# Batch 0 of a windowed-attention and SiLU-MLP kernel: scores of each head by its own half of the rows, q without padding, the first layer of tile 0 in halves of d_ff, and one more O group by DMA

## The chip, the core and the metric

The kernel runs on one core of a Trainium2 chip. The metric is the device time of one execution in microseconds (us); shorter is better. The profiles come from the hardware profiler, which records every instruction of each engine: TensorE (PE, and PEld for its weight loads), VectorE (DVE), ScalarE (ACT), GpSimd (POOL), and SyncE (SP), which here only issues DMAs.

## What is computed

Causal attention with a window of 64 positions over 8 batches of 8 heads (576 positions, head size 64), then a two-layer MLP with SiLU over all 4608 rows.

```
scores = (q @ k.T) / sqrt(64)              # per batch and head, 576 x 576
scores = where(0 <= i - j < 64, scores, -1e9)
attn   = softmax(scores)
O      = attn @ v                          # -> x: 4608 rows of 512 (8 heads x 64)
h      = x @ w_in                          # 512 -> 2048
out    = (h * sigmoid(h)) @ w_out          # 2048 -> 512, float32
```

## The kernel before

**Attention.** Heads go in pairs (`pj` = 0 to 3), one head on partitions 0 to 63 and the other on 64 to 127. q and k are turned by TensorE (`turn_heads`, L299, a pair of matmuls on the two 64-column halves of the array; `turn_twos`, L308) and copied from PSUM to SBUF ("lifts": `lift_q` L321, `lift_k` L327, `lift_twos` L314); later batches are turned by DMA transposes on SP's queue (L260), and DVE spreads q from the tile `raw` (L268). `kt` holds k for the pair, and `qbd` holds q padded: of each head only its own 64 partitions are filled, the others are zero, so that one matmul of 128 contraction rows and 128 columns gives both heads' scores for 64 queries against 128 keys. The zeros of both buffers of `qbd` are written once by ACT (`clear_q`, L215).

Nine blocks of 64 queries make three groups (`g`) of three blocks. For a pair and a group in batch 0, `scores_idle` fills one PSUM bank: first a matmul of the identity with a bias (L356, 384 columns), which masks, then three score matmuls (L361). ACT takes the exponential of 384 columns (L367). Other batches leave the bias out (`scores`, L349), and DVE multiplies with a mask (L370). Then `values` (L375) multiplies with v and its column of ones, DVE inverts the sums (L381) and scales (`normal_both` L410, or ACT L414, in batch 0; `normal` L387 in batches 1 and 2; `normal_rows` L404 from batch 3 on). O is turned into `bridge`, the MLP's input, in three ways: by matmuls with 64 columns (`back_both`, L420) in batch 0, by three matmuls of a 64-wide identity (`back`, L431) and a copy (L436) for each pair and group in batches 1 and 2, and by one DMA transpose for the four pairs of a group (`turn_o`, L425) from batch 3 on.

**MLP.** Nine tiles of 512 rows. The first layer of a tile is 64 matmuls (L440: 16 blocks `ft` of d_ff by 4 blocks of d_model) with a SiLU per `ft` on ACT (L446); the second layer is 64 matmuls of 512 columns (L449), a copy out (L455) and a store. Tile 0 begins before batch 0 is done: its first layer is made for rows 0 to 191, all 16 `ft`, and then for rows 192 to 511 (`PARTS`).

**Order.** The order of instructions on each engine comes from a planner in the kernel (`Plan`): every operation is added with a class, an engine or two, a guessed cost and its dependencies, and a list scheduler with ranks per class picks the next one for each engine. The hardware then runs each engine's list strictly in this order. PSUM has eight banks, four named `at` (attention) and four `mp` (MLP). In the first microseconds TensorE runs matmuls with no use, "warm" fillers (L680), wherever the plan has nothing else for it. All loads from DRAM except the first two go over POOL's queue, in one order: q, k and v of batch 0, w_in in 8 chunks (L278), batch 1, w_out in 8 chunks (L284), and the other batches.

Of the kernel before, what the change touches and what calls it, by code (L numbers as in the profile page):

```python
# [8 lines left out]
FP32 = mybir.dt.float32  # L9
# [102 lines left out]
def kernel(ctx, tc, q, k, v, w_in, w_out, out):  # L112
    nc = tc.nc
# [14 lines left out]
    NN, NNB, NE, NOB, NOT, NGT = 8, 8, 14, 6, 4, NFT + 3  # L128
    PARTS = {0: [(0, 192), (192, TT)]}
    NXQ, NXK, NXO = 4, 2, 3  # L130
# [23 lines left out]
    vv = [keep.tile([128, H * NB + 1, D + 2], BF16, name=f"vv{i}") for i in range(NK)]  # L154
    es = [keep.tile([128, 3, 2, 64], BF16, name=f"e{i}") for i in range(NE)]
    rcs = [keep.tile([128, 3, 2], FP32, name=f"rc{i}") for i in range(NRC)]
# [55 lines left out]

    def clear_q(i, hh):
        r = slice(64 - 64 * hh, 128 - 64 * hh)
        nc.scalar.copy(out=qbd[i][r, :, hh].bitcast(FP32), in_=zero[r].unsqueeze(2).to_broadcast([64, NP, S // 2]))  # L215

    def clear_ob(i):
# [5 lines left out]
    c_zero = p.add("one", {"DVE": 0.1}, lambda _: nc.vector.memset(zero, 0.0))  # L223
    c_q = {i: [p.add("first", {"ACT": 1.0}, lambda e, i=i, hh=hh: clear_q(i, hh), [c_zero]) for hh in range(2)]
           for i in range(NK)}
    c_twoi = p.add("late", {"DVE": 0.3}, const_twoi, [c_ident])
# [65 lines left out]

    def turn_heads(op, w, hs):

        pst = at_bf16(op).rearrange("x (m p) -> x m p", m=NM)
        heads = natbs[w].rearrange("p (h m d) -> p h m d", h=2, m=NM)
        for m in range(NM):
            for hh in hs:
                nc.tensor.matmul(  # L299
                    pst[64 * hh:64 * hh + 64, m], lhsT=heads[:, hh, m], rhs=ident[0:NR, 0:NR],  # L300
                    is_transpose=True, start=(m == 0), stop=(m == NM - 1),
                )
# [15 lines left out]

    def lift_q(e, op, b, pj, hh):
        r = slice(64 * hh, 64 * hh + 64)  # L320
        copies[e](  # L321
            out=qbd[b % NK][r, pj, hh].rearrange("x (p m) -> x p m", m=NM),
            in_=at_bf16(op)[r].rearrange("x (m p) -> x p m", m=NM),
        )

    def lift_k(e, op, b, pj):
        copies[e](  # L327
            out=kt[b % NK][:, 64 + pj * S:64 + (pj + 1) * S].rearrange("x (p m) -> x p m", m=NM),
            in_=at_bf16(op).rearrange("x (m p) -> x p m", m=NM),
        )  # L330

# [21 lines left out]

    def scores_idle(op, b, pj, g):

        nc.tensor.matmul(  # L356
            banks[op["bank"]][:, 0:384], lhsT=ident,
            rhs=(bias0 if g == 0 else bias).rearrange("k x h i -> k (x h i)"), start=True, stop=False)
        for x in range(3):
            t = 3 * g + x  # L360
            nc.tensor.matmul(  # L361
                at_sp(op)[:, x], lhsT=kt[b % NK][:, pj * S + t * 64:pj * S + t * 64 + 128],
                rhs=qbd[b % NK][:, pj, :, t * 64:t * 64 + 64], start=False, stop=(x == 2),
            )

    def expo(op, n):
        nc.scalar.activation(out=es[n % NE], in_=at_sp(op), func=ACTF.Exp, scale=scale)  # L367

    def masking(n, g):
# [114 lines left out]
    def add_batch_qk(b):  # L484
        pool = "at" if b else "all"
        slot, parts = {}, {0: [], 1: []}
        for pj in range(NP):
            kq_done[(b, pj)] = []
            busy = s_last.get((b - NK, pj), []) + ([c_k[b % NK]] if b < NK else [])
            for kk in range(2):  # L490
# [35 lines left out]
                else:  # L526
                    ca = [p.add("dma", {"POOL": 0.66}, lambda _, w=w, pj=pj, kk=kk: load_cast(w, b, pj, kk),
                                [natb_free.get(w)], dma=0.55 if b else 0.75)]
                by = {"ACT": 0.64, "DVE": 0.75}
                li = []  # L530

                for hs in ([(0,), (1,)] if b == 0 and not kk else [(0, 1)]):
                    twos = b > 0 and not kk
                    us = 0.27 if twos else 0.35 * len(hs)
                    tu = p.add("turn", {"PE": us}, None, ca + [c_ident] + busy, lat=0.1, pool=pool, b=b)
                    tu["fn"] = lambda _, tu=tu, w=w, hs=hs, twos=twos: turn_twos(tu, w) if twos else turn_heads(tu, w, hs)
                    if kk:
                        tu["until"] = [p.add("lift", by, lambda e, tu=tu, pj=pj: lift_k(e, tu, b, pj), [tu] + busy, b=b)]
                    elif twos:
                        for hh, r in [(0, 0), (0, 1), (1, 0), (1, 1)]:  # L540
                            tu["until"].append(p.add("lift", {"ACT": 0.44, "DVE": 0.43}, lambda e, tu=tu, pj=pj, hh=hh, r=r:
                                                     lift_twos(e, tu, b, pj, hh, r), [tu] + busy + tu["until"], b=b))
                    else:
                        for hh in hs:
                            tu["until"].append(p.add("lift", by, lambda e, tu=tu, pj=pj, hh=hh: lift_q(e, tu, b, pj, hh),
                                                     [tu] + busy + tu["until"], b=b))
                    li += tu["until"]
                natb_free[w] = tu
                kq_done[(b, pj)] += li
            if b < NIV:  # L550
# [17 lines left out]
    def add_batch_attention(b):  # L568
        pv_last[b], o_rows = [], []
        pool = "at" if b else "all"  # L570
        for g, pj in [(g, pj) for pj in range(NP) for g in range(NG)] if b < NPM else [(g, pj) for g in range(NG) for pj in range(NP)]:
# [3 lines left out]
                if b == 0:  # L575
                    pool = "at" if pj >= 2 and g else "all"
                s = p.add("s" + ahead, {"PE": 0.17 if b else 0.4}, None,
                          kq_done[(b, pj)] + g_pv[n - NE:n - NE + 1] * (n >= NE) + ([] if b else c_bias) + c_q.get(b, []),
                          lat=0.1, gate=scores_may_run, pool=pool, b=b)
                s["fn"] = lambda _, s=s, pj=pj, g=g: (scores if b else scores_idle)(s, b, pj, g)  # L580
                s_last[(b, pj)] = [s]
                ex = p.add("exp" + ahead, {"ACT": 0.5}, lambda _, s=s, n=n: expo(s, n), [s], table="exp", b=b)
                s["until"] = [ex]
                exps.setdefault(b, []).append(ex)
                ma = ex
                if b:
                    ma = p.add("mask", {"DVE": 0.37}, lambda _, n=n, g=g: masking(n, g), [ex, *c_mask], b=b)
                pv = p.add("pv" + ahead, {"PE": 0.17}, None,
                           [ma] + v_done[(b, pj)] + g_back[n - NOB:n - NOB + 1] * (n >= NOB and 0 < b < NXO), lat=0.1, pool=pool, b=b)
                pv["fn"] = lambda _, pv=pv, n=n, pj=pj, g=g: values(pv, n, b, pj, g)  # L590
# [4 lines left out]
                by = {"DVE": 0.37}  # L595
                if b >= NXO:
                    no = [p.add("norm" + ahead, by, lambda e, pv=pv, n=n, hh=hh: normal_rows(pv, n, hh),
                                [rc] + xo.get(n // NP - 2 * NOX, []), b=b) for hh in range(2)]
                    g_norm.append(no[1])
                    pv["until"] = no  # L600
                    o_rows += no
                    if pj == NP - 1:
                        xo[n // NP] = [p.add("xo", {"SP": 1.4}, lambda _, n=n, g=g: turn_o(n, b, g), o_rows, dma=1.6)]
                        o_done[NG * b + g] = xo[n // NP]
                        o_rows = []
                    g_back.append(None)
                    continue
# [19 lines left out]
    def add_tile(j):  # L627
        gt = {}
        parts = PARTS.get(j, [(0, TT)])
        for ft in range(NFT):  # L630
            gt[ft] = (n_gt[0] % NGT, [])
            n_gt[0] += 1
        left = NFT * NDC * len(parts)
        for lo, hi in parts:
            have = [op for i in range((j * TT + hi + 191) // 192) for op in o_done[i]]
            for ft in range(NFT):
                g, si = gt[ft]
                bank = None
                for c in range(NDC):
                    op = p.add("moe", {"PE": 0.0036 + (hi - lo) / 2400}, None,  # L640
                               have + [win[ft // 2]] + (exps[0] if j == 0 else []), lat=0.1,
                               pool=None if c else "mp")
                    bank = bank or op
                    op["fn"] = lambda _, bank=bank, ft=ft, c=c, lo=lo, hi=hi: first_layer(bank, j, ft, c, lo, hi)
                    moe.append((op, 1, left if left % (NFT * NDC) == 0 else -1))
                    left -= 1
                si.append(p.add("silu", {"ACT": 0.18 + (hi - lo) * 0.00083}, lambda _, bank=bank, g=g, lo=lo, hi=hi:
                                silu(bank, g, lo, hi), [op] + free_gt.get(g, []), table="silu"))
                bank["until"] = [si[-1]]
# [35 lines left out]
    for f in range(8):  # L685
        win.append(p.add("dma", {"POOL": 0.8}, lambda _, f=f: load_w_in(f), dma=1.33))
    add_batch_attention(0)

    p.add("prime", {"ACT": 0.2}, lambda _: nc.scalar.activation(out=spare, in_=zero, func=ACTF.Silu), [c_zero] + exps[0],
          table="silu")  # L690
    n_tile = 0
    for b in range(1, B):
# [43 lines left out]
```

## Time and profile before

| | us |
|---|---|
| median of 5 runs | 315.72 |
| lowest and highest | 315.37, 318.21 |
| the profiled execution's own time | 315.77 |
| its span in the profile | 313.7 |
| first matmul of the MLP (L440) starts | 22.09 |
| first matmul of the second layer of tile 0 (L449) starts | 42.23 |
| TensorE busy | 307.8 |
| ACT, DVE busy | 192.5, 158.4 |

The profiled execution spends 315.77 - 313.7 = 2.07 us outside the span. In the timelines each line has the start in us from the span's start, the busy time in us, the engine, the line of the kernel, the operation, out<-in by tile names, sizes, and how many instructions were merged; in brackets stands the idle time of the engine before it and what ended it. Matmuls overlap in their pipeline, so the busy time of a group is longer than the distance from its start to the next start; that distance is what TensorE spends on it. A matmul's weight load is a separate instruction (PEld) and runs beside earlier matmuls.

### The profile page before, as it was taken

The page shows a single profiled execution, that of the slowest core. Times are in us where ns is not written, and L with a number is a line of the kernel's source. Part 1 is how long each engine was busy: PE and PEld are TensorE (multiplying, and loading weights), DVE is VectorE, ACT ScalarE, POOL GpSimd, SP SyncE. Part 2 cuts the span into 40 slices and gives each one's busy share as a digit, 9 for nine tenths or more (in the row PEclk, how much of TensorE's full clock was granted, in tenths as well). Part 3 has the DMA queues.
Part 4 walks back from the last instruction along what each step waited for, and adds up shares of the span by engine and source line. Part 5 has one row for each costly group of instructions (what it writes and reads, how often), then busy time and mean ns, then how long its engine had stood idle before and what let it go on. Part 6 is the DMA issues. An engine that isn't in the chain of part 4 may idle for free.

```text
span 313.7 us, 6059 instructions
## 1 busy us (share of the span) xinstructions
PE 307.8 (98%) x2235; PEld 167.9 (54%) x2235; DVE 158.4 (50%) x471; ACT 192.5 (61%) x374; POOL 119.1 (38%) x159
## 2 busy tenths in 40 slices
PE   8999999999999999999999999999999999999995
PEld 4778666545665556545654464446444444444444
DVE  4894838945689898990895089408810000000000
ACT  8898686889867666277617761876186136316611
POOL 8956859576657769672455000000000000000000
PEclk9999999999999999999999999999999999999999
DMA  9999999999999999999999955200520110020011
GB/s 143 159 195 188 182 201 163 118 236 143 156 187 163 155 153 163 154 180 157 156 178 193 157 83 119 59 0 36 117 60 2 67 67 2 25 76 33 2 67 67
DMA packets 137308, 37.31 MB, mean 119 GB/s; under 512 B 121664, under 2 KB 132800, under 8 KB 137280
## 3 DMA queue, kind: packets, MB, share of 16 engines
q0 software_dynamic: 95712, 18.06, 74.8%
q1 hardware_dynamic: 41568, 18.88, 33.8%
q8 instruction: 17, 0.28, 0.4%
q14 instruction: 11, 0.09, 0.1%
HBM read 36.70 MB, written 9.44 MB: 147 GB/s over the span
## 4 chain that ended last, share of the span: by engine, by line
PE 93%; DVE 4%; ACT 1%; issue 0%; POOL 0%; POOLq 0%; ACTq 0%; DVEq 0%
PE mp L449 39%; PE mp L440 37%; PE at L375 5%; PE at L349 5%; DVE qbd L314 2%; PE at L680 1%; PE mp L680 1%; PE at L308 1%; DVE vv L335 1%; ACT qbd L314 1%; PE at L431 1%; PE at L420 0%; PE at L299 0%; DVE vv L337 0%; PE mp L299 0%
## 5 line engine op out<-in xcount | busy, mean ns | idle before, releaser
L449 PE MATMUL mp<-w_out_sb,g 128*128 128x512 bf16 (+2 forms) x608 | 144.7, 367 | 0.0
L440 PE MATMUL mp<-bridge,w_in_sb 128*128 128x512 bf16 (+2 forms) x640 | 131.2, 358 | 1.0 <-ACT g L446 0.8
L446 ACT ACTIVATE g<-mp 128x512 bf16<-128x512 f32 (+2 forms) x160 | 86.1, 556 | 29.8 <-PE mp L440 29.3
L440 PEld LDWEIGHTS <-w_in_sb 128*128 128x128 bf16 x640 | 60.0, 98 | 59.8 <-issue 1.6
L449 PEld LDWEIGHTS <-g 128*128 128x128 bf16 x608 | 54.6, 97 | 42.5
L455 ACT COPY ot<-mp 128x512 f32<-128x512 f32 (+2 forms) x32 | 17.8, 560 | 70.6 <-PE mp L449 65.2
L404 DVE TENSOR_TENSOR ox<-at,rc 64x192 bf16<-64x192 f32 x120 | 42.3, 353 | 2.3
L367 ACT ACTIVATE e<-at 128x384 bf16<-128x384 f32 x90 | 38.9, 496 | 7.4 <-PE at L349 6.7
L370 DVE TENSOR_TENSOR e<-e,mask 128x384 bf16<-128x384 bf16 x84 | 26.7, 349 | 30.1 <-ACT e L367 29.3
L254 POOL DMA_DIRECT2D nat<-in_k_dram x48 | 35.0, 733 | 18.1 <-DMA vv<-in_v_dram 8.2
L272 POOL DMA_DIRECT2D vv<-in_v_dram x32 | 33.5, 1052 | 15.6 <-PE at L375 9.0
L375 PEld LDWEIGHTS <-e 128*128 128x128 bf16 x288 | 22.5, 97 | 15.4 <-DVE e L370 3.1
L375 PE MATMUL at<-vv,e 128*128 128x130 bf16 x273 | 29.8, 219 | 0.0
L254 POOL DMA_DIRECT2D nat<-in_q_dram x32 | 23.8, 749 | 9.3 <-DMA vv<-in_v_dram 4.5
L349 PE MATMUL at<-qbd,kt 128*128 128x128 bf16 x252 | 23.4, 219 | 0.0
L349 PEld LDWEIGHTS <-kt 128*128 128x128 bf16 x252 | 18.2, 98 | 9.7 <-issue 1.3
L381 DVE RECIPROCAL rc<-at 128x6 f32<-128x6 f32 x91 | 17.6, 194 | 9.4 <-PE at L375 7.2
L314 DVE COPY qbd<-at 64x288 bf16<-64x288 bf16 x26 | 12.5, 480 | 11.3 <-ACT qbd L314 7.7
L387 DVE TENSOR_TENSOR ob<-at,rc 64x192 bf16<-64x192 f32 x48 | 16.8, 349 | 1.0
L268 DVE COPY qbd<-raw 64x1152 bf16<-64x1152 bf16 x16 | 9.4, 585 | 8.3 <-DMA raw<-nat 8.0
L314 ACT COPY qbd<-at 64x288 bf16<-64x288 bf16 x22 | 10.5, 476 | 3.2 <-DVE qbd L314 2.8
L235 POOL DMA_DIRECT2D natb<-in_q_dram x15 | 10.0, 670 | 3.9 <-PE at L375 1.4
(69 smaller groups left out, 162.9 us busy)
## 6 DMA issues: line engine op xcount, KB each, us to landing
out_dram<-ot SPq DMA_DIRECT2D x35, 256.0 KB, 2.3
vv<-in_v_dram POOLq DMA_DIRECT2D x32, 144.0 KB, 7.5
nat<-in_k_dram POOLq DMA_DIRECT2D x48, 72.0 KB, 7.3
nat<-in_q_dram POOLq DMA_DIRECT2D x32, 72.0 KB, 7.7
natb<-in_q_dram POOLq DMA_DIRECT2D x15, 144.0 KB, 6.4
w_in_sb<-in_moe_w_in_dram POOLq DMA_DIRECT2D x8, 256.0 KB, 8.7
w_out_sb<-in_moe_w_out_dram POOLq DMA_DIRECT2D x8, 256.0 KB, 7.9
natb<-in_k_dram POOLq DMA_DIRECT2D x7, 144.0 KB, 5.8
```

Of the source, the lines that this page charges most:

```text
L254: nc.gpsimd.dma_start(out=rows(i)[:, pj % 2, :, 64 * hh:64 * hh + 64], in_=(q, k)[kk][b, 2 * pj + hh].rearrange("(m p) d -> p m d", p=NR),)
L272: queue[e].dma_start(out=vv[b % NK][:, 2 * g0 + 1:2 * g1 + 1:2, 0:D], in_=v[b].rearrange("h s d -> (h s) d").rearrange("(g p) d -> p g d", ...
L314: copies[e](out=qbd[b % NK][64 * hh:64 * hh + 64, pj, hh].rearrange("x (p m) -> x p m", m=NM)[:, :, r::2], in_=at_bf16(op)[64 * r:64 * r + ...
L349: nc.tensor.matmul(at_sp(op)[:, x], lhsT=kt[b % NK][:, pj * S + t * 64:pj * S + t * 64 + 128], rhs=qbd[b % NK][:, pj, :, t * 64:t * 64 + 6 ...
L367: nc.scalar.activation(out=es[n % NE], in_=at_sp(op), func=ACTF.Exp, scale=scale)
L370: nc.vector.tensor_mul(es[n % NE], es[n % NE], mask0 if g == 0 else mask)
L375: nc.tensor.matmul(at_pv(op)[:, x], lhsT=es[n % NE][:, x].rearrange("p h i -> p (h i)"), rhs=vv[b % NK][:, s:s + NB + 1:NB, 0:D + 1], star ...
L404: nc.vector.tensor_mul(ox(n)[:, :, r], pv[r, :, hh, 0:D], rc[r, :, hh:hh + 1].to_broadcast([64, 3, 64]))
L440: nc.tensor.matmul(banks[bank["bank"]][:, lo:hi], lhsT=w_in_sb[:, c, ft * 128:(ft + 1) * 128], rhs=bridge[:, (j * TT + lo) // 64:(j * TT + ...
L446: nc.scalar.activation(out=gts[gt][:, lo:hi], in_=banks[bank["bank"]][:, lo:hi], func=ACTF.Silu)
L449: nc.tensor.matmul(banks[bank["bank"]][:, 0:hi - lo], lhsT=gts[gt][:, m * 128:(m + 1) * 128], rhs=w_out_sb[:, f, lo:hi], start=(f == 0), s ...
L455: copies[e](out=ots[ot][:, lo:hi], in_=banks[bank["bank"]][:, 0:hi - lo])
```

## The change

Four things change.

1. Scores of batch 0. A pair and a group no longer share a bank between heads. For each head, a bank takes group 0 (192 columns) and another takes groups 1 and 2 (384 columns). The bias matmul stays (192 or 384 columns); each score matmul contracts only over the 64 partitions of its head, and gives 64 columns. ACT takes the exponential of a bank with 192 or 384 columns and writes every second block of 64 of the `e` tiles, which are now slices of one tile `eall`.
2. q of batch 0 is not padded: it is turned like k (one turn of 12 matmuls instead of two of six) and lifted by one copy of 128 partitions instead of two of 64. The first `clear_q` of buffer 0 goes; since batch 2 uses this buffer padded, DVE writes its zeros after batch 0's scores, with two memsets of 64x1152 words.
3. Tile 0's first layer is made in four parts: `ft` 0 to 7 for rows 0 to 191 and 192 to 511, then `ft` 8 to 15 for the same two.
4. The last O group (g = 2) of batch 2 is turned by one DMA transpose (`normal_rows`, `turn_o`), as in later batches, instead of by `back` and `to_bridge` for each pair.

```diff
-    PARTS = {0: [(0, 192), (192, TT)]}
+    PARTS = {0: [(a, z, *f) for f in ((0, 8), (8, NFT)) for a, z in ((0, 192), (192, TT))]}
...
-    es = [keep.tile([128, 3, 2, 64], BF16, name=f"e{i}") for i in range(NE)]
+    eall = keep.tile([128, NE, 3, 2, 64], BF16, name="eall")
+    es = [eall[:, i] for i in range(NE)]
...
+    def lift(e, op, t):
+        copies[e](out=t.rearrange("x (p m) -> x p m", m=NM), in_=at_bf16(op).rearrange("x (m p) -> x p m", m=NM))
...
-    def scores_idle(op, b, pj, g):
-
-        nc.tensor.matmul(
-            banks[op["bank"]][:, 0:384], lhsT=ident,
-            rhs=(bias0 if g == 0 else bias).rearrange("k x h i -> k (x h i)"), start=True, stop=False)
-        for x in range(3):
+    def scores_head(op, pj, hh, g, n):
+
+        bank = banks[op["bank"]]
+        nc.tensor.matmul(bank[:, 0:192 * n], lhsT=ident, start=True, stop=False,
+                         rhs=bias0[:, :, 0] if g == 0 else bias.rearrange("k x h i -> k (x h i)")[:, 0:192 * n])
+        r = slice(64 * hh, 64 * hh + 64)
+        for x in range(3 * n):
             t = 3 * g + x
             nc.tensor.matmul(
-                at_sp(op)[:, x], lhsT=kt[b % NK][:, pj * S + t * 64:pj * S + t * 64 + 128],
-                rhs=qbd[b % NK][:, pj, :, t * 64:t * 64 + 64], start=False, stop=(x == 2),
+                bank[:, 64 * x:64 * x + 64], lhsT=kt[0][r, pj * S + t * 64:pj * S + t * 64 + 128],
+                rhs=qbd[0][r, pj, 0, t * 64:t * 64 + 64], start=False, stop=(x == 3 * n - 1),
             )
...
+    def expo_head(op, u, hh, n):
+        nc.scalar.activation(
+            out=eall[:, u:u + n, :, hh].rearrange("k u x i -> k (u x) i"),
+            in_=banks[op["bank"]][:, 0:192 * n].rearrange("k (x i) -> k x i", i=64), func=ACTF.Exp, scale=scale)
...
-                if b >= NXO:
+                if b >= NXO or (b, g) == (NXO - 1, NG - 1):
...
+    c_q[2] = [p.add("clear", {"DVE": 1.3}, lambda e, hh=hh: clear_q(e, 0, hh), [x for i in range(NP) for x in s_last[(0, i)]] + [prime])
+              for hh in range(2)]
```

The guessed costs of the touched operations change with it, and so does the planner's order on every engine.

## The prediction

> **What bounds the kernel now.** I read the page first, then the busy time in three stretches cut at the first matmul of each MLP layer, then the timelines around these cuts.
>
> ```profile
> PE 307.8 (98%) x2235; PEld 167.9 (54%) x2235; DVE 158.4 (50%) x471; ACT 192.5 (61%) x374; POOL 119.1 (38%) x159
> DMA  9999999999999999999999955200520110020011
> PE 93%; DVE 4%; ACT 1%; issue 0%; POOL 0%; POOLq 0%; ACTq 0%; DVEq 0%
> ```
>
> TensorE is busy and nearly alone on the chain of waits. The DMA row says that the engines are loaded until about 180 us.
>
> ```profile
> 7.94:22.09 14.15, 13.76 (x239) 10.22 (x239) 12.48 (x33) 12.80 (x33) 11.18 (x15) 1.00 1.52 176
> 22.09:42.23 20.14, 19.31 (x239) 14.58 (x237) 12.12 (x29) 16.22 (x45) 14.11 (x20) 1.00 1.51 188
> 42.23:310.50 268.27, 268.13 (x1735) 139.70 (x1732) 130.55 (x390) 156.11 (x291) 86.68 (x109) 1.00 1.05 111
> ```
>
> Columns: stretch, length, busy PE, PEld, DVE, ACT, POOL (each with its count), clock, DMA, GB/s. From 42.23 on TensorE never stops. So the end moves by three things: when the first layer starts, what TensorE does and waits for until 42.23, and work taken off it later. In the first stretch TensorE, ACT and DVE are all nearly full.
>
> ```profile
> 7.52 0.49 PE L680 MATMUL mp<-ident 128*128 128x384 bf16 x2
> 7.94 0.56 PE L299 MATMUL mp<-ident,natb 96*64 96x96 bf16 x12
> ...
> 17.03 0.34 PE L356 MATMUL mp<-bias,ident 128*128 128x384 bf16 x1
> 17.21 0.33 PE L361 MATMUL mp<-qbd,kt 128*128 128x128 bf16 x3
> 17.38 0.33 PE L356 MATMUL mp<-bias,ident 128*128 128x384 bf16 x1
> ...
> 22.09 0.82 PE L440 MATMUL mp<-bridge,w_in_sb 128*128 128x192 bf16 x8
> 22.84 0.28 PE L420 MATMUL at<-ident,ox 128*64 128x64 bf16 x6
> 23.05 0.67 PE L440 MATMUL mp<-bridge,w_in_sb 128*128 128x192 bf16 x6
> ...
> 38.08 0.47 ACT L314 COPY qbd<-at 64x288 bf16<-64x288 bf16 x1 [0.73 <-DVE qbd L314]
> 39.06 0.70 PE L440 MATMUL mp<-bridge,w_in_sb 128*128 128x320 bf16 x4 [0.66 <-ACT g L446]
> ...
> 47.53 0.25 PE L431 MATMUL at<-twoi,ob 128*128 128x64 bf16 x3
> 47.62 0.33 PE L349 MATMUL at<-qbd,kt 128*128 128x128 bf16 x3
> ```
>
> Starts give what TensorE spends: a bank of scores 0.35 us (17.03 to 17.38), a 64-column matmul 0.03 (47.53 to 47.62 for three). A change of tile shape shows too: eight 192-column matmuls take 8 x 0.0825 = 0.66, so L420 could start at 22.75 and starts at 22.84; its three pairs take 0.09, so L440 could start at 22.93 and starts at 23.05. Each change costs about 0.1 us.
>
> **1a. Scores by heads: TensorE.** Taken off: 12 banks of 0.163 + 3 x 0.056 = 0.33, 3.97 us. Added per pair: two banks of 0.082 + 3 x 0.0285 and two of 0.163 + 6 x 0.0285, 1.00; four pairs, 4.0. So the streams are equal. What is new is that each bank goes from a full-array matmul (bias) to tiles of 64 rows and back. In the order of instructions of both kernels I counted changes of tile shape between the first turn and the first L440: 26 before, 49 after. 23 x 0.1 = +2.3 us.
>
> The trace shows such changes for halves of the columns only. The Trainium skill (TensorEngine Tiling, Key Properties) says that a change of tiling mode drains the array; it gives no price and excepts no shape, so I take the row's 0.1 for row tiles too. Its Theoretical Speedup table promises up to 2x for a contraction of 64 or less: by it the 72 matmuls would take 1.0 instead of 2.05. I don't count it: the three or six of a bank all sit on the same half.
>
> A second rule speaks against the change. TensorE: Matmul & The Clock Gate, What overlaps and what doesn't (in its Part 3), says that a weight load overlaps running matmuls only when the row groups differ. Here they do not. By the rule each of 72 matmuls pays its load, 97 ns by the PEld rows, so 72 x (0.097 - 0.0285) = +4.9 us. But the L431 row is a case of the same row group with 64 columns and a new weight each time, and runs at 0.03: the load is hidden. I take the row, and keep +4.9 as the upper end; the lower is 0, or -1.0 by the table.
>
> **1b. Scores by heads: ACT.** Exponentials of 384 columns follow each other at 0.38 us (three in 1.25 at 20.05), 192-column SiLUs at 0.25 (two in 0.56 at 24.19). From 12 x 0.38 = 4.6 to 8 x 0.38 + 8 x 0.25 = 5.0: +0.5. One tile `eall` for all slots could add false waits: the listed waits of these exponentials name the same engines as before, so 0 (at most a few tenths).
>
> **2. q unpadded.** ACT's lifts of batch 0 go from seven to three, 4 x 0.63 = -2.5; DVE keeps five of 0.75. So ACT is relieved by 2 us and TensorE becomes the bound of this stretch. The two clears gone from ACT (1.16 each) free it before the casts, but the first turn at 7.94 stands behind 30 fillers, which end there (row at 7.52), and still does: 0. DVE gets two memsets; 218 ns for 192 words in the L218 row makes 1.25 for 1152, 2.5 in all. They stand after batch 0's last bridge copy, where DVE now idles 2.3 us before its first lift at 28.19. Their waits (batch 0's scores, the dummy SiLU) are over by then. The cover is just used up: 0 to 0.5 us late; if it is gone, the lifts come up to 2.5 later and ACT's SiLUs behind them.
>
> First L440: TensorE's work from 7.94 on, before: turns 2.0, scores 4.0, values 2.1, turns back 0.7, nine fillers 1.5, changes 2.6: 12.9 of 14.15, so 1.25 of waiting. After: +2.3 changes, +0.16 for one filler more: 15.4. All waiting absorbed gives 23.3, none 24.6; I take 23.6, **+1.5**.
>
> **3. Parts of tile 0, and the stretch to L449.** Its work does not change: 64 x 0.0825 + 64 x 0.1357 = 13.96, turns 2.0, turns back 0.35, scores 0.7, 16 changes 1.6: 18.6 of 20.14, so 1.5 us are waits. Most are at 38 to 40: ACT stands in a lift that waits for DVE's, the SiLUs queue behind, and L440 has no bank. A start 1.5 later finds batch 1's q and k landed when their turns come (by the view of `natb`, the first issued at 17.4 takes 10.1 to land, 27.5; the last at 29.8 takes 5.8, 35.6). The new parts move the 320-column matmuls to between the turns, which gives ACT time. I keep 0.3 of the waits (between 0 and 1.5, and with late clears up to 3): **-1.2**. w_in's chunks are needed no earlier. L449 would start at 42.5.
>
> **4. Group 2 of batch 2 by DMA.** Off TensorE: 12 matmuls of L431, 12 x 0.03 = **-0.35**. Off ACT and DVE: four copies of 0.32; the eight scalings (349 against 353 ns) are level. POOL's list is unchanged. SP gets a transpose of about 1.2 us between a `kt` transpose and a store; the store has slack, as it frees one of four `ot` buffers. The result is needed by tile 3's first layer at about 132 us, over 25 us later.
>
> ```profile
> 180.31 0.36 DVE L370 TENSOR_TENSOR e<-e,mask 128x384 bf16<-128x384 bf16 x1 [2.91 <-ACT e L367]
> 180.70 0.75 DVE L337 COPY vv<-vv 64x2304 bf16<-64x2304 bf16 x1
> ...
> 182.30 0.34 PE L375 MATMUL at<-vv,e 128*128 128x130 bf16 x3
> DMA to landing us min/median/max: 11.5/11.5/11.5
> ```
>
> Its transfer loads the queues. The last line is the last load of batch 7's v, issued at 168.8: it lands at 180.3, and DVE's shift of v follows at 180.70, with the mask for L375 at 182.30 queued behind. Slack: 0.4 there, and 0.3 from that mask's end (181.92) to L375. A transpose takes 1.2 us or so of the stream; if all of that reaches this load, TensorE loses about 0.5 to 0.7. I take +0.2.
>
> **Sum.** +1.5 - 1.2 - 0.35 + 0.2 = +0.15 us on the profiled execution's 315.77, that is 315.9; this execution is 0.05 above the median, so 315.8.
>
> **Rivals.**
> - *Weight loads of row tiles are not hidden.* Place: the 72 score matmuls before the first L440; price +4.9, less 0.3 of waiting absorbed: 315.8 + 4.4 = 320.2. It decides from a spacing of about 0.05 us per matmul (72 x 0.0215 = 1.6). For: the rule above, and no row of 64-row tiles. Against: L431.
> - *The SiLU waits stay or grow behind the memsets.* +1.2 to +2.5: 317.0 to 318.3. For: DVE's cover is thin. Against: TensorE, too, comes later.
> - *The load of v decides at 181 us.* With all of the transpose in its way +0.5 more: 316.3.
> - *Faster: row tiles cost no change of shape.* 32 changes go, L440 starts near 22, but then batch 1's loads (27.5 to 35.6) hold its turns, and v's landing takes what exceeds the slack of 0.7: 314.9. Below 314.2 needs the loads to come earlier too.
>
> **Chances.** 0.5% is 1.6 us, about what a measurement of this kernel can tell from no change. My forecast 0.50, the v load 0.13: both within. Faster rival 0.12, of which 0.07 beyond 1.6 us. SiLU waits 0.10, half beyond. Unhidden loads 0.15, all beyond. Faster 0.07, same 0.73, slower 0.20. The range 314.5 to 318.2 leaves out most of the unhidden loads above and a little below.
>
> **What would show it.** Right: scores' tiles 0.03 us apart with 0.1 at each end; first L440 at 23.3 to 24.6; L449 at about 42.5; no L440 waiting for ACT at 38 to 40; twelve fewer L431; the v load landing at 180.3 or later. Wrong: score matmuls 0.1 apart, L440 after 26, or L449 before 41.5.

## The result, and the profile after

| | before | after |
|---|---|---|
| median of all executions | 316.46 us (79) | 320.23 us (44) |
| lowest, highest | 314.7, 322.21 | 315.94, 322.81 |
| executions above 318 us | 16 of 79 | 32 of 44 |
| ratio, 95% interval | | 1.0064 [1.0047, 1.0081] |
| span of the profiled execution | 313.7 | 320.1 |

The change makes the kernel slower: by 2.0 us by the ratio, by 3.8 us by the medians. The two differ because the ratio, here and in the table of the experiments, leaves out executions that are over 1.5% above the fastest of their kernel, and the profiled execution of after (322.15 us) is one of these. What makes an execution long turns out to be the subject of this case, so the counts above 318 us are given as well. That line is a coarse one: of the 32 of after above it, 23 took over 320 us, with a mean granted clock of 0.995 or less, and the other nine ran at 1.00.

The page of after, with the lines for engines, clock, DMA and the chain of waits:

```profile
PE 311.7 (97%) x2264; PEld 169.4 (53%) x2264; DVE 157.3 (49%) x469; ACT 189.6 (59%) x372; POOL 118.9 (37%) x159
...
PEclk9999999999999999999999979999999999999999
DMA  9999999999999999999999933400340120020012
...
PE 93%; DMA 4%; DVE 1%; issue 1%; POOL 0%; POOLq 0%; ACT 0%; DVEq 0%; ACTq 0%
```

Two things are new. The chain holds 4% of DMA, where before had none, and the granted clock has a dent in one slice of 8 us, the 24th, which begins at 184. Busy time in the three stretches of the prediction, cut at the same instructions as before (first turn, first L439, first L448; the edit has moved the lines L440 and L449 to L439 and L448):

```profile
8.63:24.48 15.85, 15.85 (x280) 10.86 (x279) 12.22 (x33) 12.33 (x33) 11.04 (x15) 1.00 1.51 184
24.48:43.36 18.88, 18.88 (x239) 14.71 (x237) 14.14 (x31) 14.98 (x44) 13.54 (x19) 1.00 1.45 177
43.36:316.57 273.21, 269.70 (x1723) 140.18 (x1720) 127.75 (x386) 156.92 (x291) 86.49 (x109) 0.99 1.06 109
```

Against before: the first turn starts 0.69 later, the first stretch is 1.70 longer, the second 1.26 shorter, the third 4.9 longer. The last number is the loss, and the timeline shows its place:

```profile
182.91 0.38 PE L448 MATMUL mp<-w_out_sb,g 128*128 128x512 bf16 x1
185.39 0.75 DVE L330 COPY vv<-vv 64x2304 bf16<-64x2304 bf16 x1 [3.89 <-DMA vv<-in_v_dram]
...
186.29 0.32 DVE L369 TENSOR_TENSOR eall<-eall,mask 128x384 bf16<-128x384 bf16 x1
...
186.66 0.35 PE L374 MATMUL at<-vv,eall 128*128 128x130 bf16 x3 [3.37 <-DVE eall L369]
```

DVE stands 3.89 us in front of the shift of batch 7's v, because the last of its loads lands at 185.3 (before: 180.3). The mask of batch 6 is queued behind the shift, L374 waits for the mask, and TensorE, which takes its list in order, waits with it. It is the place that the prediction named; it was priced there at +0.2 us, or 0.7 at most. The stop also costs clock. Busy time in three windows around it, first of after, then of before:

```profile
182.90:186.60 3.70, 0.39 (x5) 0.05 (x1) 1.18 (x4) 0.61 (x2) 0.00 (x0) 1.00 1.07 135
186.60:190.40 3.80, 3.74 (x21) 2.30 (x22) 2.39 (x8) 1.80 (x4) 0.00 (x0) 0.55 0.18 69
190.40:200.00 9.60, 9.60 (x65) 5.03 (x64) 8.40 (x28) 1.72 (x4) 0.00 (x0) 1.00 0.30 78
```

```profile
182.90:186.60 3.70, 3.70 (x34) 2.35 (x33) 3.37 (x11) 2.13 (x5) 0.00 (x0) 1.00 0.31 97
186.60:190.40 3.80, 3.80 (x26) 1.98 (x24) 3.46 (x12) 0.59 (x1) 0.00 (x0) 1.00 0.50 110
```

After the stop the granted clock (the column after POOL's) is 0.55 for 3.8 us, so 3.8 x 0.45 = 1.7 us more are lost. The stop itself is 3.4 us (L374 row): 3.4 + 1.7 = 5.1; less 0.3 for the L431 work that is gone, 4.8 of the 4.9. The Trainium skill (TensorE: Matmul & The Clock Gate, Part 1) says that the clock falls to half after an idle window of about 3.4 us. The stops of 3.4 us here and of 3.5 us in x3 below agree. But a stop of 2.9 us in x7 was enough too (its granted clock is 0.51 from 101.60 to 105.05), and one of 1.2 us in x11 left the clock at 1.00. So less than the page's figure is enough here; where the line lies is not shown.

The scores by heads look as predicted. The timeline of after:

```profile
11.70 0.26 PE L350 MATMUL mp<-bias,ident 128*128 128x192 bf16 x1
11.89 0.26 PE L355 MATMUL mp<-qbd,kt 64*128 64x64 bf16 x3
12.08 0.34 PE L350 MATMUL at<-bias,ident 128*128 128x384 bf16 x1
12.35 0.34 PE L355 MATMUL at<-qbd,kt 64*128 64x64 bf16 x6
12.63 0.34 PE L350 MATMUL mp<-bias,ident 128*128 128x384 bf16 x1
```

A bank of 192 columns takes 12.08 - 11.70 = 0.38, one of 384 takes 0.55. The streams alone would be 0.082 + 3 x 0.0285 = 0.17 and 0.163 + 6 x 0.0285 = 0.33. Each bank pays 0.2 for its two changes of tile shape. The weight loads of the 64-row tiles are hidden: three matmuls are followed by the next bank after 0.19 (11.89 to 12.08), six after 0.28 (12.35 to 12.63), so three more cost 0.09.

### The profile page after: what moved, and what is told of

The parts are those of the page before. It is cut to its first block, busy times and chain, and to the rows that moved or that the text cites. A ratio compares the mean times of both kernels' runs of the same rounds, so it can differ in the third digit from the quotient of the medians.

```text
span 320.1 us, 6115 instructions
## 1 busy us (share of the span) xinstructions
PE 311.7 (97%) x2264; PEld 169.4 (53%) x2264; DVE 157.3 (49%) x469; ACT 189.6 (59%) x372; POOL 118.9 (37%) x159
## 4 chain that ended last, share of the span: by engine, by line
PE 93%; DMA 4%; DVE 1%; issue 1%; POOL 0%; POOLq 0%; ACT 0%; DVEq 0%; ACTq 0%
PE mp L448 38%; PE mp L439 37%; PE at L374 5%; PE at L342 4%; DMA vv<-in_v_dram 4%; PE at L679 2%; PE mp L679 1%; PE at L302 1%; PE mp L355 1%; PE at L311 1%; PE mp L350 1%; PE at L419 1%; PE at L430 0%; DVE ob L386 0%; PE mp L374 0%
## 5 line engine op out<-in xcount | busy, mean ns | idle before, releaser
L448 PE MATMUL mp<-w_out_sb,g 128*128 128x512 bf16 (+2 forms) x608 | 146.0, 370 | 0.0
L439 PE MATMUL mp<-bridge,w_in_sb 128*128 128x512 bf16 (+2 forms) x640 | 130.4, 358 | 0.1
L439 PEld LDWEIGHTS <-w_in_sb 128*128 128x128 bf16 x640 | 60.2, 98 | 59.4 <-issue 0.4
L448 PEld LDWEIGHTS <-g 128*128 128x128 bf16 x608 | 55.0, 98 | 42.7
L454 ACT COPY ot<-mp 128x512 f32<-128x512 f32 (+2 forms) x34 | 19.0, 561 | 72.0 <-PE mp L448 62.4
L403 DVE TENSOR_TENSOR ox<-at,rc 64x192 bf16<-64x192 f32 x128 | 45.1, 352 | 2.5
L257 POOL DMA_DIRECT2D nat<-in_k_dram x48 | 36.5, 765 | 19.6 <-DMA nat<-in_k_dram 10.0
L361 ACT ACTIVATE eall<-at 128x384 bf16<-128x384 f32 x84 | 36.1, 497 | 10.2 <-PE at L342 9.7
L369 DVE TENSOR_TENSOR eall<-eall,mask 128x384 bf16<-128x384 bf16 x84 | 26.5, 350 | 30.6 <-ACT eall L361 29.8
L275 POOL DMA_DIRECT2D vv<-in_v_dram x32 | 32.2, 1014 | 13.9 <-PE at L374 7.6
L374 PE MATMUL at<-vv,eall 128*128 128x130 bf16 x276 | 29.4, 219 | 3.4 <-DVE eall L369 3.4
L374 PEld LDWEIGHTS <-eall 128*128 128x128 bf16 x288 | 22.4, 97 | 19.1 <-DVE eall L369 6.8
L386 DVE TENSOR_TENSOR ob<-at,rc 64x192 bf16<-64x192 f32 x40 | 14.0, 349 | 0.8
```

Of the source, the lines that this page charges most:

```text
L257: nc.gpsimd.dma_start(out=rows(i)[:, pj % 2, :, 64 * hh:64 * hh + 64], in_=(q, k)[kk][b, 2 * pj + hh].rearrange("(m p) d -> p m d", p=NR),)
L275: queue[e].dma_start(out=vv[b % NK][:, 2 * g0 + 1:2 * g1 + 1:2, 0:D], in_=v[b].rearrange("h s d -> (h s) d").rearrange("(g p) d -> p g d", ...
L369: nc.vector.tensor_mul(es[n % NE], es[n % NE], mask0 if g == 0 else mask)
L374: nc.tensor.matmul(at_pv(op)[:, x], lhsT=es[n % NE][:, x].rearrange("p h i -> p (h i)"), rhs=vv[b % NK][:, s:s + NB + 1:NB, 0:D + 1], star ...
L403: nc.vector.tensor_mul(ox(n)[:, :, r], pv[r, :, hh, 0:D], rc[r, :, hh:hh + 1].to_broadcast([64, 3, 64]))
L439: nc.tensor.matmul(banks[bank["bank"]][:, lo:hi], lhsT=w_in_sb[:, c, ft * 128:(ft + 1) * 128], rhs=bridge[:, (j * TT + lo) // 64:(j * TT + ...
```

## The experiments

| | kernel | median us | before beside it | ratio to before, 95% | above 318 us |
|---|---|---|---|---|---|
| x1 | after without part 4 | 317.96 | 316.30 | 1.0033 [1.0013, 1.0053] | 11 of 22 |
| x2 | after, late shift of batch 7's v | 316.36 | 316.30 | 1.0013 [0.9998, 1.0027] | 0 of 22 |
| x3 | before + part 4 | 320.41 | 316.30 | 1.0010 [0.9978, 1.0041] | 18 of 22 |
| x4 | before, late shift | 315.91 | 316.30 | 0.9990 [0.9977, 1.0004] | 0 of 22 |
| x5 | x4 + part 4 | 315.33 | 315.90 | 0.9976 [0.9962, 0.9990] | 0 of 22 |
| x6 | x5, copy for the transpose | 315.25 | 315.90 | 0.9975 [0.9963, 0.9987] | 0 of 22 |
| x7 | x4 + three O groups by DMA | 320.80 | 315.90 | 1.0148 [1.0117, 1.0179] | 4 of 4 |
| x8 | x4 + parts 1, 2 | 316.93 | 315.90 | 1.0029 [1.0017, 1.0041] | 0 of 22 |
| x9 | x3, copy for the transpose | 315.79 | 316.13 | 0.9993 [0.9955, 1.0031] | 3 of 12 |
| x10 | x2, 20 fillers | 315.02 | 316.13 | 0.9962 [0.9946, 0.9979] | 0 of 12 |
| x11 | x4 + parts 3, 4 | 316.13 | 316.13 | 0.9990 [0.9974, 1.0006] | 0 of 12 |
| x12 | x5, 20 fillers | 315.07 | 316.13 | 0.9965 [0.9952, 0.9978] | 0 of 7 |
| x13 | x2, 16 fillers | 314.64 | 315.74 | 0.9967 [0.9953, 0.9981] | 2 of 14 |
| x14 | x13 without part 3 | 315.96 | 315.74 | 1.0003 [0.9992, 1.0015] | 2 of 14 |

Where kernels that ran at different times are compared below, each is taken against the kernel before that ran beside it.

### Is it the order of DVE? (x2, x4)

The edit of both makes the planner place the shift of batch 7's v later; no operation is added and POOL's list stays the same.

```diff
-                        lv[a:z], b=b) for hf in range(2)]
+                        lv[a:z] + (pv_last[b - 1] if b == B - 1 else []), b=b) for hf in range(2)]
```

> The changed kernel, with one edge more in the planner: the shift of batch 7's v waits for the last value product of batch 6, so that it is placed at about 197 us in DVE's order instead of 181, and the masks of batch 6 no longer stand behind it. Loads and transposes are the same. If the loss is DVE's order (the landing of v in front of the masks): the loads may land as late as 185 and TensorE does not notice; no stall between 180 and 200, 315.8 + 0.8 = 316.6, nearly the same in every execution, so about 3.5 us under the changed kernel's median. If the loss at 180 to 190 is something else that only shows there (the exponentials, the transposed q of batch 7): it stays at 319 to 321.

Measured: 316.36, and no execution above 318. In x2's profile the last load of v lands at 185.2, as late as in after, and nobody waits. Its timeline at the place where after stood:

```profile
183.16 0.32 DVE L369 TENSOR_TENSOR eall<-eall,mask 128x384 bf16<-128x384 bf16 x1
183.38 0.34 PE L374 MATMUL at<-vv,eall 128*128 128x130 bf16 x3
```

> The kernel before, with the shift of batch 7's v placed late in DVE's order as above and nothing else. Before has 0.7 us of slack at this place, so its profiled time should stay (315.7, within 0.3), but a fifth of its executions lie above 318. If these are executions in which the same load lands late, they vanish: all within 315.2 to 317.2. If they have another cause, a fifth still lies above 318.

Measured: 315.91, all within 315.01 to 316.62. So the long executions of before are the same stop: they vanish when no mask stands behind the shift. (Before had only 6 of 75 beside x4, so 22 executions could miss them by luck. But of the eight kernels with the late shift, x7 apart, that have 20 fillers or more, none of 141 executions is above 318, against 13 of 164 of before beside them.) The loss of after is DVE's order meeting a late load. Without it after is 0.06 above before, x4 is 0.39 below: parts 1 to 4 cost 0.45 us.

### What makes the load late? (x1, x3, x9)

x1 takes part 4 out of after, x3 puts it alone into before.

```diff
-                if b >= NXO:
+                if b >= NXO or (b, g) == (NXO - 1, NG - 1):
```

> The changed kernel with its fourth part undone: the last O group of batch 2 goes through TensorE and twoi again, and SP issues no transpose for it. In the changed kernel's profile TensorE stands 3.5 us at 182.9 behind DVE's shift of batch 7's v, whose load lands at 185.3 (180.3 before the change), and runs its next matmuls at a lower clock: 5.3 us lost between 180 and 200. Theory A (the added transpose's traffic makes that load late): the load lands at 181 to 182, the stall is gone or under 1 us, and the time is that of before plus what the trace shows at 180 us, 0.83, plus 0.3 for the L431 work given back: 316.5 to 317.2. Theory B (the load is late because the later and heavier first 45 us push the whole list of loads back, the transpose has little to do with it): it still lands near 185, the stall of 3 us or more stays, and the time stays at 319 to 321.

> The kernel before, with the fourth part alone: the last O group of batch 2 by DMA. My prediction gave this part -0.35 for the twelve matmuls and +0.2 for the load of v at 181 us, so -0.15 (315.6). Theory A (the transpose's traffic makes the load late, by up to 5 us): v lands at 183 to 185, TensorE stands 1.5 to 3.5 us, and the time is 317 to 320.5. Theory B (the load is late because of the first 45 us): the load stays at 180 to 181, 315.3 to 315.8.

18 of x3's 22 executions are above 318, 16 of them with a granted clock of 0.995 or less; of before beside it, six of 75 are, all at 0.995 or less. Its profile shows the stop of after without any of parts 1 to 3: the landing is at 185.3, and these are two rows of its timeline and the third stretch of its busy times (first L449 to the end), 5.2 us longer than before's 268.27:

```profile
185.46 0.76 DVE L337 COPY vv<-vv 64x2304 bf16<-64x2304 bf16 x1 [4.06 <-DMA vv<-in_v_dram]
...
186.73 0.35 PE L375 MATMUL at<-vv,e 128*128 128x130 bf16 x3 [3.54 <-DVE e L370]
```

```profile
43.21:316.64 273.43, 268.38 (x1698) 140.15 (x1720) 127.93 (x386) 156.95 (x291) 86.21 (x108) 0.99 1.04 109
```

x3's four shortest executions (314.58 to 316.07) show what part 4 does when the load is in time. x1, with parts 1 to 3 and no transpose, lies between: its profiled execution had the load at 181.5 and a stop of 0.2, but 11 of its 22 are above 318. Five of these (318.04 to 318.59) ran at a clock of 0.998 to 1.00; six (321.28 and more) have the 0.995 of the long stop, against six of 75 of before. So theory A is right about x3 and only half right about x1: parts 1 to 3 seem to raise the odds as well, by less than the count above 318 suggests. That they do it by starting the later work later (first L448 at 43.36 against 42.23) is an argument, no measurement: in x1's own profile it is at 42.43.

> The kernel before with part 4, its transpose replaced by four plain DMAs on SP that move the same 768 pieces of 256 bytes (the transposition is left out, so tile 3 gets other data), and without the late shift, so that the times show how often the v load is late: above 318 us lay 17 of 22 executions of the kernel before with part 4, and about 1 in 7 of the kernel before. Theory T (the transpose as such holds up the loads): about as the kernel before, at most 5 of 22 above 318, median 315.8. Theory P (any 768 more packets, or SP's list): 12 or more of 22 above 318, median 318.5 or more.

The edit of x9 (x6 has it too) replaces the transpose of that group:

```diff
         n0, i = b * NB + 3 * g, n // NP
+        if b < NXO:
+            rows_in = oxs[i // 2 % NOX][64 * (i % 2):64 * (i % 2) + 64].rearrange("i t j x -> i (t j) x")
+            for z, c in ((0, 0), (0, 1), (1, 0), (1, 1)):
+                nc.sync.dma_start(
+                    out=bridge[64 * z:64 * z + 64, n0:n0 + 3].rearrange("x t (c j) i -> x c t (j i)", c=2)[:, c],
+                    in_=rows_in[:, 6 * z + 3 * c:6 * z + 3 * c + 3])
+            return
         nc.sync.dma_start_transpose(
```

Measured: 315.79, three of twelve above 318 (theory T), where before beside it had four of 30. The profiled execution is one of the three: its load lands at 183.5 and TensorE stops for 3.4 us, so the stop needs no added transpose. Twelve executions can't tell the copies' odds from before's; with the transpose the odds are four in five (18 of 22; the 17 in the expectation was a miscount). By these counts it is the transpose itself that does most of the harm, not the 768 packets and not SP's list.

The transpose does not meet the late load directly. In after it is issued at 100.6 and has landed at 107.9, and the load of v is issued over 60 us later. The issues of batch 7's v, first and last start, in before and then in after:

```profile
L272 POOL DMA_DIRECT2D vv<-in_v_dram x4: 986/1108/1327, 164.7 to 168.8; - x4
L275 POOL DMA_DIRECT2D vv<-in_v_dram x4: 983/992/995, 168.0 to 172.1; - x4
```

So 3.3 of the 5.0 us are there when the load is issued, and 1.7 come on its way (13.2 us from issue to landing, against 11.5). POOL's list, between 95 and 176 us, stands 20.2 us behind landings of earlier loads in after, 18.4 in x3 and 16.5 in before: the lateness adds up over many loads. How the transpose starts it is not shown.

### How much does a transpose cost the stream? (x5, x6, x7)

> The kernel before with the late shift of batch 7's v and part 4 (last O group of batch 2 by DMA): the part's worth where nothing on TensorE waits for the v load. Kernels without the part landed their last v load at 180.3 to 181.9 us, kernels with it at 185.2 to 185.3. Theory A (the late landing was the whole harm): it lands near 185 again, no stall follows, and the time is that of the late-shift kernel, 315.9, less 0.3 for the twelve matmuls: 315.6. Rival (the twelve matmuls were hidden, or the later loads bite elsewhere): 315.9 or more.

> As the kernel with the late shift and part 4, but the group's transpose is replaced by four plain DMAs on SP at the same place that move the same 768 pieces of 256 bytes from the same rows into the same place of bridge; the transposition itself is left out, so tile 3 gets other data. Theory T (the transpose as such holds up the stream of loads): the last v load lands at 180 to 182 as without the part. Theory P (it is the additional packets, or SP's shifted list): it lands at 184 to 186 as with the transpose. Time 315.6 in both, as nothing waits for it.

The times came as expected: x5 is 0.57 below before, x4 0.39, so part 4 alone is worth 0.2 by the medians. In the busy times of x5 the third stretch is 0.3 shorter than before's:

```profile
42.98:310.97 267.99, 266.47 (x1698) 139.50 (x1720) 128.51 (x386) 156.77 (x291) 86.26 (x108) 1.00 1.05 111
```

The landings did not come as expected: 180.5 in the profile of x5, with the transpose, and 183.5 in that of x6, with the copy. x8 below, without either, has 185.1. One profile shows one draw. Across all sixteen profiles the last load landed between 176.5 and 187.3. In the nine with the one added transpose it landed at 180.5 (x5) and at 183.3 to 187.3 (the other eight); in the four with neither transpose nor copies at 180.3 to 181.9 and at 185.1 (x8). The groups lean apart but overlap, so only the counts of executions tell. How the transpose shifts the odds, packet by packet, stays open.

> The kernel before with the late shift and all three O groups of batch 2 by DMA (two transposes more than part 4, 24 matmuls of L431 less): the price of a transpose by a larger dose. If one costs the stream about 4 us each time, the last v load lands at 185 + 2 x 4 = 193; if it costs its own 1.3 us of the 16 engines, at 188; if the 4 us were one slot lost once, at 185 to 186. The time is 315.6 - 0.6 = 315.0 if nothing else becomes late, and 316 or more if batch 7's q and k or tile 2's input do.

x7 moves all three groups of batch 2 (`b >= NXO - 1` in the condition). It missed every landing: the load lands at 176.5, earlier than in any other profile. It is issued at 171.4, as late as elsewhere, but is under way for 5.1 us only, where the others take 11.3 to 13.3; why is open. The time is 320.8, as the expectation's last clause has it for the case that tile 2's input is late. Its timeline shows that wait:

```profile
100.54 0.82 PE L440 MATMUL mp<-bridge,w_in_sb 128*128 128x512 bf16 x3 [2.90 <-DMA bridge<-ox]
```

Tile 2's first layer needs groups 0 and 1 of batch 2, and by DMA they come 2.9 us too late; the clock falls after this stop as well. Group 2, which part 4 moves, has tile 3 as its reader and time to spare. A price per transpose can't be read from x7.

### The start: parts 1, 2, 3 and the fillers (x8, x10 to x14)

> The kernel before with the late shift and parts 1 and 2 alone (scores by heads, q unpadded), tile 0's parts as before. Against the late-shift kernel (315.9): from the first turn to the first L440 +1.5 us (16.0 against 14.3 in the profiles so far). Theory M (the later start, not the new order of tile 0's parts, takes out the waits between the first L440 and L449): that stretch falls from 19.9 to about 18.9, so +0.5: 316.4. Theory N (the new parts do it): it stays at 19.9 or grows behind DVE's memsets, +1.5 to +2.5: 317.4 to 318.4.

316.93, 1.03 above the kernel before, where M said 0.5 and N 1.5 or more. The profile decides for M: the stretch from the first L439 to L448 is 19.10, against 19.65 to 20.14 in the seven profiles without parts 1 to 3, so the later start takes out most of the waits.

```profile
8.78:24.56 15.78, 15.78 (x279) 10.86 (x279) 12.57 (x33) 12.34 (x33) 11.64 (x16) 1.00 1.51 185
24.56:43.66 19.10, 19.10 (x240) 14.67 (x238) 14.09 (x30) 15.25 (x45) 14.20 (x20) 1.00 1.51 191
```

> The kernel before with the late shift, part 4 and part 3 (tile 0's first layer in halves of d_ff). Without part 3 it measured 315.3. In the profiles the stretch from the first L440 to L449 is 19.9 us in kernels without parts 1 and 2 and 19.1 with them, 18.9 with part 3 on top. Theory M (the later start took the waits out): part 3 brings 0.2 or less: 315.1 to 315.4. Theory N (the new parts take the SiLU waits at 38 to 40 us out by themselves): stretch 19.0, 314.5.

The edit is the `PARTS` line and its loop from the change. 316.13, level with before, where x5 was 0.57 below: alone, part 3 costs. Both theories missed that. The stretch grew to 20.36, and its timeline still has the wait for ACT, now for longer:

```profile
37.39 0.24 PE L440 MATMUL mp<-bridge,w_in_sb 128*128 128x192 bf16 x1 [1.22 <-ACT g L446]
```

> The changed kernel with the late shift and 20 instead of 30 fillers before the first turn. In its profile ACT's casts end at 5.9 us and the first turn stands behind fillers until 8.63. If the fillers are what holds it (my step 2 said that the 2.3 us of ACT's clears gain nothing because of them): first turn at about 6.2, first L440 about 22.3 instead of 24.5, and of the 2.3 us some 0.8 is given back in the stretch to L449, as batch 1's loads come no earlier: 316.4 - 1.5 = 314.9. Rival 1: the turns then run before TensorE's clock is up, and the loads of the later pairs hold them: 0 to -0.5, 315.9 to 316.4. Rival 2: slower than 316.4 since the clock comes up later.

> Control for the fillers: the kernel before with the late shift, part 4 and 20 fillers before the first turn. Here ACT's clears end at 6.7 and its casts at 8.15 us, so the first turn cannot come much before 7.9 whatever the fillers do: first turn 7.9 to 8.2 against 7.8 to 8.7, time 315.3 within 0.3. If it gains as much as the changed kernel does, the clears were not what held the turn.

```diff
+    p.add_filler(20, "warm", {"PE": 0.255}, warm, [c_ident], gate=lambda: moe[0][0]["seen"] is None,
+                 pool="all")
     p.add_filler(60, "warm", {"PE": 0.17}, warm, [c_ident], gate=lambda: moe[0][0]["seen"] is None,
```

x10 is 1.11 below before; x2, the same with 30 fillers, was 0.06 above: 1.2 for ten fillers. Its first turn is at 7.30, not 6.2, since a filler takes 0.32 us (four from 2.62 to 3.90 in its timeline) until the clock is up. The control x12 gains too, 0.5 against x5 (1.06 below before), with its turn at 7.51, earlier than the 7.9 that the expectation gave as its limit. So by these medians about 0.7 of the 1.2 us belongs to part 2.

> The changed kernel with the late shift and 16 fillers before the first turn (20 gave 315.0 and the first turn at 7.30; a filler takes 0.32 us before TensorE's clock is up). If fillers still hold the turn: first turn at about 6.1, first L440 near 22.2, of the 1.2 us about 0.4 given back before L449: 314.2. Rival: the turns now run at the low clock and wait for the second pair's rows, which land at 7.4 to 8.3: 314.8 to 315.2.

> The same without part 3 (tile 0's first layer in two parts of columns only). In the profiles with parts 1 and 2 the stretch from the first L440 to L449 was 19.1 us without part 3 and 18.9 with it. If part 3 is worth these 0.2: 0.2 slower than the run beside it. If it costs, as it did on the kernel before (316.1 against 315.3): up to 0.8 faster. With the earlier start the SiLU waits may come back here and not beside: then 0.5 to 1 slower.

x13 uses 16 fillers of 0.32. In its timeline the first turn waits for ACT's cast and for nothing else:

```profile
4.25 1.74 ACT L250 CAST natb<-nat 96x768 bf16<-96x768 f32 x2
...
5.42 0.45 PE L302 MATMUL at<-ident,natb 96*64 96x96 bf16 x12
```

It is 1.10 below before, no better than x10, although its first L448 comes at 40.77 against 42.03. Two of its 14 executions, and two of x14's, took over 320. These four have a mean granted clock of 0.972 to 0.973, where the stop for v leaves 0.989 to 0.995, so they are another loss, or more than that stop; only the two kernels with 16 fillers have them, and none of the 19 executions with 20 fillers. Their profiled executions are short ones, so where the long ones lost the time is open. x14 shows what part 3 is worth when the start is early: it is 1.3 slower. The second stretch of x13 and then of x14:

```profile
21.75:40.77 19.02, 19.02 (x240) 14.66 (x237) 13.94 (x30) 15.39 (x45) 13.58 (x19) 1.00 1.54 191
```

```profile
22.13:42.38 20.25, 19.21 (x239) 14.58 (x237) 14.63 (x31) 14.85 (x44) 14.15 (x20) 1.00 1.48 182
```

Three versions lie about 1.1 us below before: x10, x12 and x13, the last with two long executions in 14. The smallest of them, x12, holds nothing of parts 1 to 3.

## Why the prediction was wrong, step by step

- **1a, TensorE, and the first L440 (+1.5): right.** From the first turn to the first L440 the seven profiles with 30 fillers and without parts 1 to 3 take 14.01 to 14.61 us (mean 14.25), and the five with parts 1 and 2 and at least 20 fillers take 15.78 to 16.04 (mean 15.87): +1.6. The change of tile shape at 0.1 us holds for tiles of 64 rows, and the rule that a load of the same row group is not hidden does not hold here (L355 rows). The +2.39 of the two profiled executions holds 0.69 of something else: the first turn, which with 30 fillers starts anywhere from 7.7 to 9.2 in twelve profiles.
- **2: right as far as it went.** The cover of ACT's 2.3 us was named, 30 fillers, and taking fillers away brings part of it out (x10, x12). The memsets took 1.02 us each, not 1.25, and cost nothing that shows.
- **3 (-1.2): right in size.** The stretch fell by 1.26 in the profiled pair, by 1.0 between the means of the profiles (19.89 and 18.89). The working gave it to both the later start and the new parts. The runs split it: the later start alone brings 0.8 (x8), the parts 0.2 at that start, 1.2 at an earlier one (x14), and a loss of 0.6 without parts 1 and 2 (x11).
- **4, L431 (-0.35): right.** 268.3 without part 4, 268.0 with it (third stretch of x4 and x5).
- **4, the load of v (+0.2): the step that failed.** I had the place, the slack of 0.7 and the queue behind it, and priced lateness as one number, with the transpose's own 1.2 us as its most. Three things were wrong. The landing is no number: over the profiles it spreads by several us, so a slack of 0.7 is a chance, and before already lost it in 16 of 79 executions, and in 16 of 191 beside the experiments. The 1.2 us are what SP's instruction takes (1218 ns at 187.4 in before), not the transfer: that one landed after 3.0 us, and the six that before issued between 100 and 140 us, with the engines loaded, after 4.9 to 9.3. So 1.2 was no upper limit for the lateness; in the two profiled executions the load lands 5.0 us later. And the loss is more than the wait, since the stop of 3.4 us takes the clock down as well: 5.1 us where I had 0.2. Of this rival (316.3 at 0.13) the mechanism came true and its size did not.
- The sum of the other terms was half a microsecond too low: with the stop taken away, parts 1 to 4 cost 0.45 us (x2 against x4), where I had +0.15 less the 0.2 for v.

## What to carry to other kernels

Where a profile shows a wait for a DMA with a slack of less than a microsecond in front of an engine that others queue behind, take the landing as a spread: count how many of the known times lie far above the median, as they may already be this wait being lost. An operation that waits for a transfer belongs in an engine's list where its result is needed, not where the transfer is expected, for everything behind it inherits the lateness; one dependency in the planner was worth 3.7 us of after's median. A step that is hidden now may be worth moving once its cover is known, but the cover (here the fillers) has to go with it.

## What the runs showed of the hardware

- In this kernel one more DMA transpose of 192 KB on SP's queue, while loads fill the DMA engines, makes long executions four in five, where plain DMAs of the same pieces have one in four (x3: 18 of 22, x9: 3 of 12; before beside them: 6 of 75 and 4 of 30). Alone late in the kernel a transpose is 3.1 us from issue to landing (193.4 to 196.5 in after).
- TensorE's start varies from execution to execution: in the first microseconds a matmul of 384 columns takes 0.32 us, later 0.16, and the step comes at about 5 us in before's profile, 6 in after's, 7 in x2's. With 30 fillers that moves the first turn by up to 1.4 us, as much as any part of this change.
- A stop of 3.4 us cost 1.7 us more at a clock of 0.55; the low clock ended at about 190.4, when TensorE had been busy again for some 3.7 us. A stop of 2.9 us (x7) brought the clock down as well.
